# Where a block's results wait on their way out: staging them in the attention output's buffer

## The chip, the cores and the metric

The kernel runs on one core of a Trainium2 chip. The metric is device time in microseconds (us) of one execution. Engines go by the profile's names: PE is TensorE (PEld its weight loads), DVE is VectorE, ACT is ScalarE, POOL is GpSimd, SP is the engine that issues the DMAs.

## What is computed

Three stages follow one another. First an attention over 4 batches of 8 heads: 512 local tokens each attend to a window of 32 tokens to either side and to 32 global tokens, and the 32 global tokens attend to all 544. Its 2176 rows of 512 then go through two feed-forward networks.

```python
x = attn_out.transpose(0, 2, 1, 3).reshape(2176, 512)
h = x @ w_in                                   # 512 x 2048
x = where(h > 0, h, exp(min(h, 0)) - 1) @ w_out
xn = x / sqrt(mean(x * x, -1) + 1e-6) * rms_g
out = (silu(xn @ w_gate) * (xn @ w_val)) @ w_o2   # 512 x 1536, 1536 x 512
```

Products are made in three passes of a 32-bit format, a value being split into a high and a low part (ScalarE casts the high part, VectorE subtracts it to get the low one).

## The kernel before

**Blocks.** The local tokens are four blocks, one per batch, of 512 columns each. `moe_block(b, slot)` (L312) runs block b of the first network in 16 chunks j of 128 hidden units. In each chunk `mm1` (L126) makes h with 12 matmuls, the slot function calls `act1` (L136), which makes e and from it g, and `mm2` (L143) adds the previous chunk's g to four results y0 to y3 in PSUM (12 matmuls, two halves of 6). The last chunk's `mm2` and the store of the block's results are carried into the next block's chunk 0 (`finish_block`, L305; `store_y`, L152); for block 3 they follow its loop (L899).

**Attention beside it.** While block b runs, `att_slot` (L287) does the attention of block b + 1, one tile of 128 tokens per four chunks: scores and exponentials (`a_S`, `a_E`) in the first, transposes (`a_T`, ptp and ET) in the second, the product with V and its normalisation (`a_PV`, `a_N`) in the third. `a_N` writes the result x into a tile of tag x32 that is asked for at the block's first tile (L264); its writes are L272. In chunk 15 `a_X` (L274) transposes x into the next block's input xT. The slots also decode the second network's weights (L83, L90 to L93, L483 to L486), which go back to DRAM by small stores (L459). In block 3 the slot function `slot3` (L854) does the global tokens' attention instead; it collects its output in xg32, a tile of tag x32 (L779, written by `g_X`, L852), and from chunk 10 on runs the global tile through the first network, summing it in gg["y"], a PSUM tile.

**Result store.** Four evictions in turn, ScalarE for 0 and 2 into tag stg, VectorE for 1 and 3 into tag e, and a DMA after each:

```python
if dc % 2:
    t = moe.tile([P, 512], F32, tag="e", name="yev", bufs=2)
    nc.vector.tensor_copy(t[:, :n], ys[dc][:, :n])
else:
    t = stg.tile([P, 512], F32, tag="stg", name="yev")
    nc.scalar.copy(t[:, :n], ys[dc][:, :n])
nc.sync.dma_start(out=yT[:, dc, t0:t0 + n], in_=t[:, :n])
```

**Buffers.** Tiles of one pool and tag share its buffers and get them in the order in which the program asks; whoever writes a new tile waits until all readers of the buffer's last one are done, a DMA among them. Tag e has two buffers, which hold the e of `elu` and `elu_a` (L112, L120) as well; stg has two; x32 has one; xT3 has one and holds a quarter of xT in the blocks and sq2, the squares for the second network's norm (L611), behind them.

**After block 3.** The global tile's sum is copied to ysb (L901, tag stg), transposed (`g_finish`, L718, tile ygt), copied again (L723, tag stg) and stored. Then the second network runs in three chunks of columns: `product` (L726, tiles A and Q) makes the gate and value products from weights that `split` (L571) prepares, `o_mm` (L735) the last one. The norm's sums for the next chunk are acc (L609, tag stg) and sq (L614), and L625 sums them over partitions.

**Order.** TensorE's instructions run in the order of the program. Those of the other engines and of SP, which issues every DMA and waits in order for what each needs, are ordered when the kernel is built, by a planner that works with an estimated timeline and the program's order as priority. `e`, `yev`, `x` and the others in the profile are the tiles' names.

Of the kernel before, what the change touches and what calls it, by code (L numbers as in the profile page):

```python
# [7 lines left out]
F32 = mybir.dt.float32  # L8
# [13 lines left out]
P = 128  # L22
# [20 lines left out]
def fused_kernel(ctx: ExitStack, tc: tile.TileContext, kq, vl, gkq, gv, w_in, w_out, w_gate, w_val, w_o2, rms_g, consts, out):  # L43
    nc = tc.nc
# [5 lines left out]
    stg = ctx.enter_context(tc.tile_pool(name="stg", bufs=2))  # L50
    moe = ctx.enter_context(tc.tile_pool(name="moe", bufs=1))
# [6 lines left out]
    ident = cpool.tile([P, P], F32, name="ident")  # L58
# [3 lines left out]
    yT = dram.tile([P, 4, NT], F32, name="yT")  # L62
# [87 lines left out]
        return [yps.tile([P, 512], F32, tag=f"y{i}", name=f"y{i}") for i in range(4)]  # L150

    def store_y(ys, t0, n):  # L152
        for dc in range(4):
            if dc % 2:
                t = moe.tile([P, 512], F32, tag="e", name="yev", bufs=2)
                nc.vector.tensor_copy(t[:, :n], ys[dc][:, :n])
            else:
                t = stg.tile([P, 512], F32, tag="stg", name="yev")
                nc.scalar.copy(t[:, :n], ys[dc][:, :n])
            nc.sync.dma_start(out=yT[:, dc, t0:t0 + n], in_=t[:, :n])  # L160


    SETS = ("A11", "A12", "S2", "S1", "S3", "A22", "S4")
# [14 lines left out]
    with ExitStack() as ls:  # L178
# [126 lines left out]
        def finish_block(dcs=range(4)):  # L305
            ys, g, t0, n = carry[0]
            mm2(ys, g, 15, n, dcs)
            if dcs[-1] == 3:
                store_y(ys, t0, n)
                carry.clear()  # L310
# [379 lines left out]
    def second_mm2(i):  # L690
        if i == 0:
            gg["y"] = aps.tile([P, 512], F32, tag="att", name="yg")
        if 0 <= i < 4:
            g_mm2(gg["y"], gg.pop(i), i)
# [21 lines left out]
    gg = {}  # L716

    def g_finish(ysb):  # L718
        pt = aps.tile([P, 512], F32, tag="att", name="ygt")
        for i in range(4):  # L720
            nc.tensor.transpose(pt[:, i * P:(i + 1) * P], ysb[:, i * P:(i + 1) * P], ident)
        yt = stg.tile([P, 512], F32, tag="stg", name="yev")
        nc.scalar.copy(yt, pt)  # L723
        nc.sync.dma_start(out=yT[:, :, 16 * P:17 * P], in_=yt.rearrange("p (c t) -> p c t", c=4))

    def product(ps, k, i, pos, m, first=True):  # L726
        n, q = sizes[k], 14 * i + 2 * pos + m
# [48 lines left out]
    xg = xgp.tile([P, 4, 2, P], F32R, name="xg")  # L776
    with ExitStack() as gs:
        gp = gs.enter_context(tc.tile_pool(name="gp", bufs=1))
        xg32 = moe.tile([P, 4, 512], F32, tag="x32", name="xg32")  # L779
        zero = gp.tile([P, 64], F32, name="zero")[:, 0:1]  # L780
        nc.vector.memset(zero, 0.0)
        G = {}

        def g_load_k(b):
            if b < 4:
                r = gp.tile([P, 4 * S + 4 * SG], F32, tag="gkq", name="gkq")
                nc.sync.dma_start(out=r, in_=gkq[b])  # L790
                for par in range(2):
                    G[2 * b + par] = {"k": r[:, :4 * S].rearrange("p (a n) -> p a n", a=4), "q": r[:, 4 * S:].rearrange("p (a n) -> p a n", a=4)}

        def g_load_v(u):
            if u < 8:
                r = gp.tile([P, 5, 256], F32, tag="gvr", name="gvr", bufs=2)
                nc.sync.dma_start(out=r, in_=gv[u])
                G[u]["v"] = r

        def g_S(b, n):  # L800
            ds = [G[2 * b + par] for par in range(2)]
            if n == 0:
                for d in ds:
                    d["st"] = small.tile([P, 8], F32, tag="st", name="gst")
                    d["p"] = gp.tile([P, 576], F32, tag="gp", name="gpp", bufs=4)[:, :S]
            ss = [aps.tile([P, 272], F32, tag="att", name="gs") for par in range(2)]
            for a in range(4):
                for par in range(2):
                    r = slice(64 * par, 64 * par + 64)
                    nc.tensor.matmul(ss[par][32 * a:32 * a + 32, :], ds[par]["q"][r, a, :], ds[par]["k"][r, a, n * 272:(n + 1) * 272], start=True, stop=True)  # L810
            for par in range(2):
                nc.vector.tensor_tensor_reduce(out=ds[par]["p"][:, n * 272:(n + 1) * 272], in0=ss[par], in1=zero.to_broadcast([P, 272]), scale=-SCALE, scalar=3.0e38,
                                               op0=ALU.add, op1=ALU.min, accum_out=ds[par]["st"][:, n:n + 1])
            if n == 1:
                for d in ds:
                    st, p = d["st"], d["p"]
                    nc.vector.tensor_tensor(out=st[:, 3:4], in0=st[:, 0:1], in1=st[:, 1:2], op=ALU.min)
                    nc.scalar.activation(p, p, AF.Exp, bias=st[:, 3:4], scale=-1.0, accum_out=st[:, 4:5])
                    nc.vector.tensor_scalar(out=st[:, 6:7], in0=st[:, 4:5], scalar1=1e-9, scalar2=None, op0=ALU.add)
                    nc.vector.reciprocal(st[:, 7:8], st[:, 6:7])  # L820

        def g_T(u):
            d = G[u]
            p = d["p"]
            pa = aps.tile([P, 512], F32, tag="att", name="gpa")
            pb = aps.tile([P, P], F32, tag="att", name="gpb")
            for c in range(4):
                nc.tensor.transpose(pa[:, c * P:(c + 1) * P], p[:, c * P:(c + 1) * P], ident)
            nc.tensor.transpose(pb[:32, :], p[:, 512:544], ident)
            pt = gp.tile([P, 640], F32, tag="gpt", name="gpt", bufs=2)  # L830
            nc.scalar.copy(pt[:, :512], pa)
            nc.vector.tensor_copy(pt[:32, 512:640], pb[:32, :])
            d["pt"] = pt

        def g_PV(u):
            d = G[u]
            o = aps.tile([P, 64], F32, tag="att", name="go")
            for c in range(5):
                r = P if c < 4 else 32
                for a in range(4):  # L840
                    nc.tensor.matmul(o[32 * a:32 * a + 32, :], d["pt"][:r, c * P + 32 * a:c * P + 32 * a + 32], d["v"][:r, c, 64 * a:64 * a + 64],
                                     start=(c == 0), stop=(c == 4))
            e = gp.tile([P, 64], F32, tag="ge", name="ge", bufs=2)
            nc.vector.tensor_scalar(out=e, in0=o, scalar1=d["st"][:, 7:8], scalar2=None, op0=ALU.mult)
            d["e"] = e

        def g_X(u):
            d = G.pop(u)
            b, par = u // 2, u % 2
            x = aps.tile([P, P], F32, tag="att", name="gx")  # L850
            nc.tensor.transpose(x[:64, :], d["e"], ident)
            nc.scalar.copy(xg32[64 * par:64 * par + 64, :, b * 32:b * 32 + 32], x[:64, :].rearrange("d (a q) -> d a q", a=4))  # L852

        def slot3(j, part, h):  # L854
            g = act1(h, 512) if part == 0 else None
            b = j // 2
            if j < 8:
                if j % 2 == 0:
                    if part < 2:
                        g_S(b, part)  # L860
                    elif b:
                        g_PV(2 * b - 1)
                        g_load_v(2 * b + 1)
                        g_X(2 * b - 2)
                elif part < 2:
                    g_T(2 * b + part)
                else:
                    g_load_k(b + 1)
                    g_PV(2 * b)
                    g_load_v(2 * b + 2)  # L870
                    if b:
                        g_X(2 * b - 1)
            elif j == 8 and part == 2:
                g_PV(7)
                g_X(6)
            elif j == 9 and part == 0:
                g_X(7)
                nc.scalar.copy(xg[:, :, 0, :], xg32[:, :, :P])
                nc.vector.tensor_tensor(out=xg[:, :, 1, :], in0=xg32[:, :, :P], in1=f(xg[:, :, 0, :]), op=ALU.subtract)
            elif j == 9 and part == 2:  # L880
                gs.close()
                second_start()
            if j >= 10:
                if part == 0:
                    if 0 <= j - 11 < 4:
                        gg[j - 11] = g_act(gg.pop("e"))
                    if j - 12 < 3:
                        second_mm2(j - 12)
                    second_mm1(j - 10)
                if part == 2:  # L890
                    second_slot(j - 10)
            return g

        g_load_k(0)
        g_load_v(0)
        g_load_v(1)
        moe_block(3, slot3)
        second_mm2(3)
        finish_block()  # L899
    ysb = stg.tile([P, 512], F32, tag="stg", name="ysb")  # L900
    nc.vector.tensor_copy(ysb, gg["y"])  # L901
    split()
    g_finish(ysb)
    stage.close()
# [3 lines left out]
    for k in range(3):  # L908
        n = sizes[k]
# [163 lines left out]
```

## Time and profile before

| | |
|---|---|
| runs of the kernel | 912.31 us median of 3 (911.75 to 914.02) |
| profiled execution, device time | 914.21 us |
| its span, first to last instruction | 912.3 us |
| mean granted clock of TensorE | 0.983 |
| DVE busy, ACT busy | 587.0 us (64%), 476.0 us (52%) |
| moved by DMA | 139.27 MB |

A line of the timeline has the start, the duration, the engine, the line of the kernel, the operation and out<-in; in square brackets stands the idle time of the engine just before and what ended it. SPq is SP issuing a DMA, and the duration there is the issue, not the transfer. A line of a window has the stretch, its length and each engine's busy time in it. In the chain of what ended last each piece has its start, its length and its kind; a DMA there is the time from issue to landing.

### The profile page before, as it was taken

The numbers are of one execution on the slowest core, as the hardware profiler recorded it, in microseconds if no ns is written. First come the engines' busy times: TensorE is split into PE (matmuls) and PEld (weight loads), VectorE is DVE, ScalarE is ACT, GpSimd is POOL, SyncE is SP. The second block draws the span as 40 slices with busy tenths as digits, with TensorE's granted clock in tenths as the row PEclk, the third lists the DMA queues.
The fourth block names the chain that finished last, engine by engine and source line by source line (L and its number), as shares of the span: only waits on it lengthen the run. The fifth ranks groups of instructions, "written<-read, shape, count | busy, mean of one in ns | idle before, by whom it ended". The sixth has DMA issues, their size and how long they took to land.

```text
span 912.3 us, 16268 instructions
## 1 busy us (share of the span) xinstructions
PE 870.9 (95%) x6652; PEld 741.3 (81%) x6652; DVE 587.0 (64%) x983; ACT 476.0 (52%) x863; POOL 18.5 (2%) x22
## 2 busy tenths in 40 slices
PE   4789999899999999999999799999999999999996
PEld 3567877688887888777888699997999998899985
DVE  4899978667678763543489455886355786365642
ACT  4677664345454544333456456665445665355531
POOL 0000000000000000000110100000100100000000
PEclk8999999899999999999999899999999999999999
DMA  9785365766686862351405532243122333133200
GB/s 361 279 300 203 124 239 176 260 206 220 223 300 216 256 198 110 128 191 59 165 1 184 172 94 93 93 136 118 58 93 93 113 98 102 52 123 116 93 24 35
DMA packets 60370, 139.27 MB, mean 153 GB/s; under 512 B 5000, under 2 KB 30728, under 8 KB 57736
## 3 DMA queue, kind: packets, MB, share of 16 engines
q1 hardware_dynamic: 60296, 138.24, 44.0%
q8 instruction: 52, 0.85, 0.4%
q14 instruction: 22, 0.18, 0.1%
HBM read 115.15 MB, written 23.07 MB: 152 GB/s over the span
## 4 chain that ended last, share of the span: by engine, by line
PE 75%; DVE 10%; DMA 8%; ACT 3%; issue 2%; SPq 1%; ACTq 0%; DVEq 0%
PE A L732 16%; PE o L738 15%; PE y L146 13%; PE h L132 13%; PE Q L732 11%; DMA yT<-yev 2%; DMA kq<-in_kq 2%; DMA raw<-in_moe_w_in 2%; DVE dx L92 2%; DVE dx L93 1%; PE o L257 1%; PE ptp L244 1%; DVE dx L90 1%; PE s L226 1%; PE hg L667 1%
## 5 line engine op out<-in xcount | busy, mean ns | idle before, releaser
L146 PE MATMUL y<-g,wA 128*128 128x512 f32 x768 | 200.5, 404 | 7.0 <-DVE g L140 5.2
L132 PE MATMUL h<-xT,wA 128*128 128x512 f32 x768 | 186.9, 392 | 1.7 <-DVE xT L282 1.7
L146 PEld LDWEIGHTS y<-g,wA 128*128 128x128 f32 x768 | 141.6, 191 | 43.8 <-DVE g L140 8.2
L132 PEld LDWEIGHTS h<-xT,wA 128*128 128x128 f32 x768 | 143.9, 189 | 32.9 <-DVE xT L282 2.4
L732 PE MATMUL A<-xc,wS 128*128 128x384 f32 (+1 forms) x864 | 156.8, 330 | 0.0
L732 PEld LDWEIGHTS A<-xc,wS 128*128 128x128 f32 x864 | 146.5, 189 | 3.9
L738 PE MATMUL o<-wB,p 128*128 128x512 f32 x612 | 147.4, 392 | 0.8 <-ACT p L742 0.3
L738 PEld LDWEIGHTS o<-wB,p 128*128 128x128 f32 x612 | 113.6, 188 | 24.8 <-DVE p L743 2.4
L732 PE MATMUL Q<-xc,wS 128*128 128x384 f32 (+1 forms) x648 | 115.3, 326 | 0.0
L732 PEld LDWEIGHTS Q<-xc,wS 128*128 128x128 f32 x648 | 107.8, 188 | 0.0
L587 DVE TENSOR_TENSOR wS<-wraw,wS 128x1024 fp32r<-128x1024 f32 x63 | 77.7, 1233 | 36.6 <-ACT wS L586 36.5
L747 DVE TENSOR_TENSOR t<-t,Q 128x384 f32<-128x384 f32 (+1 forms) x108 | 55.8, 527 | 39.4 <-PE Q L732 28.9
L586 ACT CAST wS<-wraw 128x1024 fp32r<-128x1024 f32 x63 | 65.9, 1050 | 18.8 <-PE Q L732 11.9
L139 ACT CAST g<-e 128x512 fp32r<-128x512 f32 x64 | 39.8, 622 | 53.7 <-DVE e L123 37.2
L121 ACT ACTIVATE e<-h 128x512 f32<-128x512 f32 x48 | 29.0, 605 | 72.1 <-PE h L132 63.6
L123 DVE SCALAR_TENSOR_TENSOR e<-e,h 128x512 f32<-128x512 f32 x48 | 32.5, 678 | 40.7 <-ACT e L122 40.7
L140 DVE TENSOR_TENSOR g<-e,g 128x512 fp32r<-128x512 f32 x64 | 43.7, 683 | 9.1 <-ACT g L139 8.8
L743 DVE TENSOR_TENSOR p<-p,p 128x384 fp32r<-128x384 f32 x36 | 19.9, 556 | 43.3 <-ACT p L742 43.3
L83 ACT ACTIVATE dx<-raw 128x1024 f32<-128x1024 f32 x34 | 39.3, 1158 | 16.2 <-DMA raw<-in_moe_w_gate 5.5
L90 DVE TENSOR_SCALAR dx<-dx 128x1024 f32<-128x1024 f32 x34 | 23.3, 689 | 34.2 <-ACT dx L83 34.0
L238 ACT ACTIVATE E<-s,mx 128x128 f32<-128x128 f32 x128 | 34.8, 385 | 17.1 <-DVE mx L236 17.1
L92 DVE SCALAR_TENSOR_TENSOR dx<-raw,dx 128x1024 int32<-128x1024 int32 x34 | 41.9, 1238 | 0.6
(173 smaller groups left out, 869.5 us busy)
## 6 DMA issues: line engine op xcount, KB each, us to landing
wraw<-wS SPq DMA_DIRECT2D x63, 512.0 KB, 3.3
raw<-in_moe_w_out SPq DMA_DIRECT2D x14, 1024.0 KB, 8.7
raw<-in_moe_w_in SPq DMA_DIRECT2D x8, 1024.0 KB, 6.2
raw<-in_moe_w_gate SPq DMA_DIRECT2D x6, 1024.0 KB, 6.1
raw<-in_moe_w_val SPq DMA_DIRECT2D x6, 1024.0 KB, 6.8
wS<-raw SPq DMA_DIRECT2D x48, 128.0 KB, 2.6
gvr<-in_gv SPq DMA_DIRECT2D x8, 640.0 KB, 4.0
wS<-dx SPq DMA_DIRECT2D x36, 128.0 KB, 2.1
```

The source lines that it names most:

```text
L83: ins = nc.scalar.activation(x, f(words(raw)[:, :, 1]), AF.Abs)
L92: nc.vector.scalar_tensor_tensor(out=i32(x), in0=word[:, :, 1], scalar=-0x40000000, in1=i32(x), op0=ALU.bitwise_and, op1=ALU.bitwise_or)
L132: nc.tensor.matmul(h[:, :n], W1[c, G][:, ws, o:o + P], xT[c][:, xs, :n], start=(k == 0), stop=(k == 11))
L139: nc.scalar.copy(g[:, 0, :n], e[:, :n])
L140: nc.vector.tensor_tensor(out=g[:, 1, :n], in0=e[:, :n], in1=f(g[:, 0, :n]), op=ALU.subtract)
L146: nc.tensor.matmul(ys[dc][:, :n], W2[j][:, ws, dc * P:(dc + 1) * P], g[:, gs, :n], start=(j == 0 and k == 0), stop=(j == 15 and k == 2))
L238: nc.scalar.activation(e[par][:, pr, :], ss[par][:, pr, :], AF.Exp, bias=mx[:, par, pr:pr + 1], scale=SCALE)
L586: nc.scalar.copy(t[:, :, 0, :], raw)
L587: nc.vector.tensor_tensor(out=t[:, :, 1, :], in0=raw, in1=f(t[:, :, 0, :]), op=ALU.subtract)
L732: nc.tensor.matmul(ps[:, :n], w[:, 2 * (q % 4) + c, ws, :], x[:, c, xs, :n], start=(first and c == 0 and z == 0), stop=(c == 1 and z == 2) ...
L738: nc.tensor.matmul(o, p[:, pp, t * P:(t + 1) * P], Wo[j][:, ww, :], start=(first and z == 0), stop=(last and z == 2))
L747: nc.vector.tensor_tensor(out=t, in0=t, in1=ps, op=ALU.add)
```

## The change

The results of blocks 0 to 2 (t0 below 1536) are evicted into one tile of tag x32 and leave by one DMA of 1 MB; block 3's leave as before. xg32 is asked for at its first use in `g_X`, behind block 2's store, instead of ahead of block 3. The global tile's sum goes into a tile of tag xT3, its copy stands ahead of `finish_block` in the program, and the transposed copy goes into the second half of the same tile.

```diff
--- before.py
+++ after.py
@@ -150,14 +150,22 @@
         return [yps.tile([P, 512], F32, tag=f"y{i}", name=f"y{i}") for i in range(4)]
 
     def store_y(ys, t0, n):
+        t = moe.tile([P, 4, 512], F32, tag="x32", name="yev") if t0 < 1536 else None
         for dc in range(4):
+            if t is not None:
+                o = t[:, dc]
+            elif dc % 2:
+                o = moe.tile([P, 512], F32, tag="e", name="yev", bufs=2)
+            else:
+                o = stg.tile([P, 512], F32, tag="stg", name="yev")
             if dc % 2:
-                t = moe.tile([P, 512], F32, tag="e", name="yev", bufs=2)
-                nc.vector.tensor_copy(t[:, :n], ys[dc][:, :n])
+                nc.vector.tensor_copy(o, ys[dc])
             else:
-                t = stg.tile([P, 512], F32, tag="stg", name="yev")
-                nc.scalar.copy(t[:, :n], ys[dc][:, :n])
-            nc.sync.dma_start(out=yT[:, dc, t0:t0 + n], in_=t[:, :n])
+                nc.scalar.copy(o, ys[dc])
+            if t is None:
+                nc.sync.dma_start(out=yT[:, dc, t0:t0 + n], in_=o)
+        if t is not None:
+            nc.sync.dma_start(out=yT[:, :, t0:t0 + n], in_=t)
 
 
     SETS = ("A11", "A12", "S2", "S1", "S3", "A22", "S4")
@@ -718,10 +726,9 @@
     def g_finish(ysb):
         pt = aps.tile([P, 512], F32, tag="att", name="ygt")
         for i in range(4):
-            nc.tensor.transpose(pt[:, i * P:(i + 1) * P], ysb[:, i * P:(i + 1) * P], ident)
-        yt = stg.tile([P, 512], F32, tag="stg", name="yev")
-        nc.scalar.copy(yt, pt)
-        nc.sync.dma_start(out=yT[:, :, 16 * P:17 * P], in_=yt.rearrange("p (c t) -> p c t", c=4))
+            nc.tensor.transpose(pt[:, i * P:(i + 1) * P], ysb[:, 0, i * P:(i + 1) * P], ident)
+        nc.scalar.copy(ysb[:, 1], pt)
+        nc.sync.dma_start(out=yT[:, :, 16 * P:17 * P], in_=ysb[:, 1].rearrange("p (c t) -> p c t", c=4))
 
     def product(ps, k, i, pos, m, first=True):
         n, q = sizes[k], 14 * i + 2 * pos + m
@@ -776,7 +783,6 @@
     xg = xgp.tile([P, 4, 2, P], F32R, name="xg")
     with ExitStack() as gs:
         gp = gs.enter_context(tc.tile_pool(name="gp", bufs=1))
-        xg32 = moe.tile([P, 4, 512], F32, tag="x32", name="xg32")
         zero = gp.tile([P, 64], F32, name="zero")[:, 0:1]
         nc.vector.memset(zero, 0.0)
         G = {}
@@ -847,6 +853,9 @@
         def g_X(u):
             d = G.pop(u)
             b, par = u // 2, u % 2
+            if u == 0:
+                G["x"] = moe.tile([P, 4, 512], F32, tag="x32", name="xg32")
+            xg32 = G["x"]
             x = aps.tile([P, P], F32, tag="att", name="gx")
             nc.tensor.transpose(x[:64, :], d["e"], ident)
             nc.scalar.copy(xg32[64 * par:64 * par + 64, :, b * 32:b * 32 + 32], x[:64, :].rearrange("d (a q) -> d a q", a=4))
@@ -875,6 +884,7 @@
                 g_X(6)
             elif j == 9 and part == 0:
                 g_X(7)
+                xg32 = G["x"]
                 nc.scalar.copy(xg[:, :, 0, :], xg32[:, :, :P])
                 nc.vector.tensor_tensor(out=xg[:, :, 1, :], in0=xg32[:, :, :P], in1=f(xg[:, :, 0, :]), op=ALU.subtract)
             elif j == 9 and part == 2:
@@ -896,9 +906,9 @@
         g_load_v(1)
         moe_block(3, slot3)
         second_mm2(3)
+        ysb = moe.tile([P, 2, 512], F32, tag="xT3", name="ysb")
+        nc.vector.tensor_copy(ysb[:, 0], gg["y"])
         finish_block()
-    ysb = stg.tile([P, 512], F32, tag="stg", name="ysb")
-    nc.vector.tensor_copy(ysb, gg["y"])
     split()
     g_finish(ysb)
     stage.close()
```

## Rows read from the trace of the kernel before

**Rows 1.** The page, its first and fourth part: busy time, and the chain that ended last

```profile
PE 870.9 (95%) x6652; PEld 741.3 (81%) x6652; DVE 587.0 (64%) x983; ACT 476.0 (52%) x863; POOL 18.5 (2%) x22
...
PE 75%; DVE 10%; DMA 8%; ACT 3%; issue 2%; SPq 1%; ACTq 0%; DVEq 0%
```

**Rows 2.** Windows: stretch, then length and busy (x instructions) by engine, clock, DMA share, GB/s

```profile
154.17:186.09 31.92, 29.08 (x242) 22.75 (x242) 18.49 (x32) 13.36 (x26) 0.00 (x0) 0.89 0.69 224
264.50:291.25 26.75, 25.81 (x242) 20.66 (x242) 18.89 (x31) 14.41 (x27) 0.00 (x0) 1.00 0.74 283
186.09:211.63 25.54, 25.54 (x242) 20.66 (x242) 18.30 (x30) 13.56 (x25) 0.00 (x0) 1.00 0.68 234
366.80:389.70 22.90, 22.90 (x228) 15.95 (x228) 11.72 (x40) 7.87 (x15) 0.00 (x0) 1.00 0.45 141
502.65:515.42 12.77, 6.52 (x29) 6.55 (x30) 3.16 (x4) 4.56 (x7) 3.00 (x3) 0.73 0.64 218
```

**Rows 3.** Timeline of ScalarE, first chunks of block 1

```profile
160.18 0.64 ACT L159 COPY yev<-y 128x512 f32<-128x512 f32 x1
160.65 1.19 ACT L83 ACTIVATE dx<-raw 128x1024 f32<-128x1024 f32 x1
167.84 0.60 ACT L121 ACTIVATE e<-h 128x512 f32<-128x512 f32 x1 [6.00 <-DMA yT<-yev]
```

**Rows 4.** Timeline of SP, first chunks of block 1

```profile
158.57 0.37 SPq L75 DMA_DIRECT2D raw<-in_moe_w_val  x1
159.50 2.25 SPq L160 DMA_DIRECT2D yT<-yev  x4
178.47 5.45 SPq L459 DMA_DIRECT2D wS<-raw  x8
```

**Rows 5.** The chain in order of time, first chunks of block 1

```profile
161.28 7.49 DMA yT<-yev
```

**Rows 6.** Timeline of ScalarE and VectorE, block 2, and ScalarE, block 3

```profile
274.62 0.60 ACT L121 ACTIVATE e<-h 128x512 f32<-128x512 f32 x1 [2.45 <-DMA yT<-yev]
...
284.72 0.75 DVE L272 TENSOR_TENSOR x<-o,st 128x256 f32<-128x256 f32 x2
...
390.67 0.24 ACT L852 COPY xg<-gx 64x128 f32<-64x128 f32 x1
```

**Rows 7.** Timeline of four engines, end of block 3

```profile
494.50 0.93 ACT L614 ACTIVATE sq<-ya 128x384 f32<-128x384 f32 x2
...
499.77 2.88 PE L146 MATMUL y<-g,wA 128*128 128x512 f32 x12
...
508.06 0.69 DVE L901 COPY ysb<-yg 128x512 f32<-128x512 f32 x1 [3.07 <-DMA yT<-yev]
...
508.89 1.09 PE L721 MATMUL ygt<-ident,ysb 128*128 128x128 f32 x4 [6.25 <-DVE ysb L901]
...
510.55 0.53 ACT L609 ACTIVATE acc<-ya 128x384 f32<-128x384 f32 x1
```

**Rows 8.** The chain in order of time, end of block 3

```profile
502.17 5.79 DMA yT<-yev
...
515.42 2.08 PE A L732 x12
```

**Rows 9.** Timeline of TensorE, first chunks of block 1

```profile
164.77 2.88 PE L132 MATMUL h<-xT,wA 128*128 128x512 f32 x12
```

**Rows 10.** Timeline of VectorE, first chunks of block 1

```profile
169.48 0.69 DVE L123 SCALAR_TENSOR_TENSOR e<-e,h 128x512 f32<-128x512 f32 x1 [4.93 <-ACT e L122]
...
171.88 0.69 DVE L140 TENSOR_TENSOR g<-e,g 128x512 fp32r<-128x512 f32 x1
...
178.15 0.75 DVE L272 TENSOR_TENSOR x<-o,st 128x256 f32<-128x256 f32 x2
```

**Rows 11.** DMA issues, 156 to 176: count, KB each, median us to landing

```profile
raw<-in_moe_w_val SPq DMA_DIRECT2D x1, 1024.0 KB, 5.3
```

**Rows 12.** The line L625 from 505 to 620: duration ns, first and last start

```profile
L625 PE MATMUL ms<-acc,ones x4: 485/486/486, 565.3 to 585.1; 128*128 128x384 f32 x4
```

## The prediction

> **What bounds the kernel now.** I read the page first. TensorE is busy 95% of the span, and the chain that ended last is 75% TensorE, 10% VectorE, 8% DMA [rows 1]. So a change that computes nothing less can only win where TensorE stands still or runs at its lower clock, and the question is where that is and whether a result store stands behind it. The windows answer it [rows 2]. In the middle of a block four chunks take 25.54 us with TensorE busy throughout at a granted clock of 1.00. The same four chunks, when they are the first of block 1, take 31.92 us, and as the first of block 2 they take 26.75 us. They hold the same work, as the matmul counts 242, 242 and 242 show. The excess is 6.38 us and 1.21 us. At block 1 TensorE's busy time is 29.08 us, so 2.84 us of the excess is idle and 3.54 us is the lower level of the clock (a mean of 0.89). At block 3 the matching stretch is wholly busy, 22.90 of 22.90 us at clock 1.00, so there is nothing to win.
>
> The timeline of ScalarE says what is late. At block 1 it ends a weight decode at 160.65 + 1.19 = 161.84 and then stands 6.00 us until a store of yev lands; only then does the next e (L121) start [rows 3]. The reason is in the code: two of the four staging tiles of store_y are taken from tag e, which has two buffers, so the next e needs the buffer of a store that is still under way. The stores are issued from 159.50 on, behind a weight load at 158.57 [rows 4], and the last is on the chain for 7.49 us, until 168.77 [rows 5]. At block 2 the same wait is 2.45 us [rows 6]; there TensorE has enough queued to hide most of it.
>
> The fourth place is the end of block 3. The last y matmuls end at 499.77 + 2.88 = 502.65, and the transposes of ygt start at 508.89 after 6.25 us of idle time [rows 7]. They wait for ysb, which VectorE copies at 508.06 after 3.07 us of waiting for a store [rows 7]; that store is on the chain from 502.17 for 5.79 us [rows 8]. Here ysb wants a buffer of tag stg, whose two buffers hold results on their way out. The window 502.65 to 515.42 holds four transposes and two groups of 12 products [rows 2]. One such group takes 2.08 us at clock 1.00 [rows 8], and four transposes about half of their 1.09 us, which ran at the lower clock; so the work is 0.55 + 2 x 2.08 = 4.71 us, and 12.77 - 4.71 = 8.06 us are lost, of which 6.2 us idle and the rest clock.
>
> **The change, part by part.** *Results of blocks 0 to 2 in x32.* The four evictions stay, on the same engines and with the same shapes (0.64 us for ScalarE's second at 160.18 [rows 3]); only their target moves. No new e waits for a store. At block 1 the e could start at 161.84, 6.00 us sooner, its h being done by then, since TensorE was well before the next one at 164.77 [rows 9]. Then VectorE's e (L123), 169.48 before, and the g that the next y needs (L140, 171.88 before) come 6 us sooner, at about 163.5 and 165.9 [rows 10]. TensorE ends its h at 164.77 + 2.88 = 167.65 [rows 9], so g is there in time, with some 1 us to spare after its 0.69 us. ScalarE's second decode lies between e and g; its weights were asked for at 158.57 [rows 4] and land 5.3 us later [rows 11], at 163.9, and the decode needs 1.2 us, so it too ends in time, but without much room. I therefore take back 5.4 of the 6.38 us at block 1 and 0.9 of the 1.21 us at block 2, and keep the whole and nothing as bounds.
>
> *One store for four.* Four issues cost SP 2.25 us in all [rows 4]; one is bounded by a single 256 KB issue (0.56 us) and by those 2.25 us. SP is on no critical path there, so I count nothing. But the one store cannot leave before the fourth eviction is done, 160.18 + 0.64 = 160.82, while the first of the four left at 159.50. What stands behind it on SP in this stretch is only later loads. The bytes are the same and the queue is full, so I take its landing to be where the last of the four landed, 168.77 [rows 5]; bounds are 0.5 us sooner and 2 us later.
>
> *The new wait that this brings.* x32 has one buffer. The attention's result for the next block but one (x, L272) goes into it, so L272 now waits for the 1 MB store, and VectorE's whole queue waits behind it: g, e and the decode. Before, L272 ran at 178.15 [rows 10]; with the 6.00 us gone it is due at about 172.2. The landing at 168.77 leaves 3.4 us. At block 2 it ran at 284.72, 10 us after the e at 274.62, whose start shows the store of its buffer landed [rows 6]. In block 3 the first write to xg32, which is now allocated after the store, is ScalarE's at 390.67 [rows 6], 24 us after the block's first chunk began at 366.8 [rows 2]. So the cost is nothing, hidden by the decode that stands before L272 on VectorE; where that cover fails it is the third rival.
> The Trainium skill (DMA: Bandwidth & Descriptors, section Anatomy of one DMA) fits a transfer by about 2.0 us plus its bytes at 436 GB/s. By that page 1 MB would be out 4.4 us after 160.82, at 165.2, and the margin would be 7 us; the rows do not agree, since a quarter of the bytes took 7.49 us in a loaded queue, and the measured landing stands in the sum. The third rival would be less likely by the page.
>
> *ysb in tag xT3, its copy written ahead of finish_block.* yg is complete when the y matmuls start at 499.77. VectorE can copy it between its weight splits, in 0.69 us [rows 7], before 502.65 in most orders; it may push an eviction back by 0.69 us, which nobody waits for. The transposes then follow the y matmuls directly and the products follow them, without the idle time behind which the clock was at its lower level. That is worth the 8.06 us as an upper bound.
> Two buffers pass to other waits, though. With ysb and the last yev gone from stg, acc of the next chunk (L609, 510.55 before [rows 7]) is the next in that tag, after the yev store that lands at 507.96 [rows 8]. And the squares sq2, of which ScalarE wrote two at 494.50 [rows 7], now come after ysb in tag xT3, so they wait for the store of ysb's second half. Their results are only needed by TensorE's L625 at 565.3 [rows 12], so they are not urgent themselves. The queue behind them is: if ScalarE stands at acc until 508.0, the copies of the first products (L921) stand behind. The products start at about 503.2, and after four groups of half-sets, 4.16 us, TensorE needs those copies, at 507.4; the two copies (0.5 us each) would end at 509. That would cost 1.6 us, and standing at sq2 up to 3.5 us. I take 1.0 us and expect 7.0 of the 8.06 us.
>
> **Sum.** 5.4 + 0.9 + 7.0 = 13.3 us. The profiled execution took 914.21 us (span 912.3), so it would become 900.9; it lies 1.9 us above the median of the runs shown, 912.31. Against that median I predict 899.0 us. With everything taken back (15.65 us) it is 896.7. Behind each of the four places TensorE is the bound, wholly busy in the windows of a block's middle and at block 3 [rows 2] and back to back in the products [rows 8], so what is won early stays won.
>
> **Rivals.** *First: block 1 gives nothing back.* ScalarE's next decode or VectorE's backlog takes the place of the store. For it: the decode has 1 us of room, and VectorE is 10% of the chain [rows 1]. Against it: VectorE itself stood idle before L123 at 169.48 for 4.93 us [rows 10]. Time: 899.0 + 5.4 = 904.4.
> *Second: the end wait changes its owner.* ScalarE stands at acc or sq2 with the copies behind it, 3.5 us rather than 1.0: 901.5, and at most 4.5 us back, so 903.
> *Third, slower.* The order of SP, ScalarE and VectorE is planned at build from an estimated timeline, so the 1 MB store may be put behind work that is blocked, such as the put group that SP issues from 178.47 to 183.92 [rows 4]. It would then leave at 184 and land some 6 us later (between 5.79 and 7.49 [rows 5, 8]), at 190. L272 would hold VectorE from 172 to 190, and TensorE, which the g already made feeds for three groups of 2.7 us, would stand from about 181 to 190.5. That is 9.5 us at each of blocks 1 and 2, with 3.5 us of clock behind each (as block 1 lost now), in place of the 6.38 and 1.21 us of now [rows 2]: 912.3 - 7.0 + 2 x 13.0 - 7.6 = 923.7. It turns the sum against the change when each of the two stands costs 8.7 us with its clock, which is a landing at about 186. Against it: before, the stores leave within 2 us of the evictions at all three boundaries.
> *Fourth: nothing happens,* since the planner's new order gives elsewhere what is won here: 912.
>
> **How the numbers follow.** The forecast has 0.64, the first rival 0.10, the second 0.12, the third 0.07, the fourth 0.07. The range reaches from everything taken back, less the 1 us by which the runs shown spread downward (895.5), to the first rival and a little of it together with the second (906.5); that leaves out the third and the fourth and a part of what may come from a new order. A measurement of this kernel can tell 0.3% (2.7 us) from no change. Faster by more than that takes the forecast, the first and second rivals and a part of the fourth: 0.88; same 0.05; slower 0.07.
>
> **What would show it.** Right: no wait of e (L121) for yT at 161.84, the first four chunks of block 1 in about 26.5 us at clock 1.00, ygt directly behind the last y, L272 without a DMA wait. Wrong: a DMA wait before L272 or acc with TensorE idle behind it; a first stretch of block 1 still near 32 us, then with a weight load or the decode as what ends the wait; the 1 MB store late on SP.

## The result, and the profile after

The changed kernel takes 898.9 us (median of 5 runs, 897.99 to 901.6) against 912.31 us for the kernel before (5 runs, 911.6 to 914.16). The ratio is 0.9853, with a 95% interval of 0.9834 to 0.9872. The forecast was 899.0 us.

The profiled execution took 899.1 us with a span of 897.3 us, 15.0 us under that of before. Its page answers to [rows 1]; TensorE's share rises, and the DMA part of the chain is halved:

```profile
PE 864.9 (96%) x6652; PEld 736.4 (82%) x6652; DVE 588.0 (66%) x983; ACT 475.8 (53%) x863; POOL 19.4 (2%) x22
...
PE 79%; DVE 11%; DMA 4%; ACT 3%; issue 1%; SPq 0%; POOL 0%; ACTq 0%
```

The windows answer to [rows 2], cut at the same instructions (first scores to the scores four chunks on for blocks 1 and 2; the whole stretch of block 3). Columns are as there.

```profile
153.19:178.75 25.56, 25.56 (x242) 20.66 (x242) 18.37 (x32) 13.48 (x26) 0.00 (x0) 1.00 0.83 271
257.16:282.70 25.54, 25.54 (x242) 20.66 (x241) 19.50 (x33) 14.48 (x27) 0.00 (x0) 1.00 0.78 292
...
358.30:381.20 22.90, 22.90 (x228) 15.97 (x227) 11.68 (x40) 7.92 (x15) 0.00 (x0) 1.00 0.42 143
```

Block 1's first four chunks take 25.56 us in place of 31.92, block 2's 25.54 in place of 26.75, both with TensorE busy throughout at clock 1.00. Block 3's stretch is what it was, 22.90 us. The timeline of block 1, all engines, shows the wait gone:

```profile
159.21 0.64 ACT L164 COPY yev<-y 128x512 f32<-128x512 f32 x1
159.68 1.20 ACT L83 ACTIVATE dx<-raw 128x1024 f32<-128x1024 f32 x1
159.87 0.65 SPq L168 DMA_DIRECT2D yT<-yev  x1
...
160.69 0.68 ACT L121 ACTIVATE e<-h 128x512 f32<-128x512 f32 x1
...
165.84 0.69 DVE L140 TENSOR_TENSOR g<-e,g 128x512 fp32r<-128x512 f32 x1
...
172.13 0.75 DVE L280 TENSOR_TENSOR x<-o,st 128x256 f32<-128x256 f32 x2
```

ScalarE starts e (L121) at 160.69, as the decode before it is ending, with no wait for yT; before it stood there 6.00 us [rows 3]. The 1 MB store leaves at 159.87, 0.02 us after the last eviction (159.21 + 0.64). Its landing is not in the profile's lists (the page's 5.5 us for such stores is the one issued at 366.57, in block 3); the last of its 16 completion events in the trace is at 167.34, 7.47 us after the issue. The attention's result x (now L280) is written at 172.13, 4.8 us later, and VectorE waits for no store there. The end of block 3 answers to [rows 7]:

```profile
491.25 2.88 PE L146 MATMUL y<-g,wA 128*128 128x512 f32 x12
...
493.27 0.68 DVE L910 COPY ysb<-yg 128x512 f32<-128x512 f32 x1
...
494.01 0.66 PE L729 MATMUL ygt<-ident,ysb 128*128 128x128 f32 x4
...
495.76 0.48 ACT L931 COPY t<-A 128x384 f32<-128x384 f32 x1
...
499.90 0.52 ACT L617 ACTIVATE acc<-ya 128x384 f32<-128x384 f32 x1 [3.65 <-DMA yT<-yev]
500.33 0.46 ACT L931 COPY t<-A 128x384 f32<-128x384 f32 x1
500.81 1.28 ACT L937 ACT_TABLE_LOAD   x1
...
500.84 1.32 PE L739 MATMUL A<-xc,wS 128*128 128x384 f32 x6 [0.94 <-ACT t L931]
...
502.10 0.53 ACT L937 ACTIVATE t<-t 128x384 f32<-128x384 f32 x1
502.53 1.04 ACT L594 CAST wS<-wraw 128x1024 fp32r<-128x1024 f32 x1
...
503.47 0.93 ACT L622 ACTIVATE sq<-ya 128x384 f32<-128x384 f32 x2
...
504.31 0.46 ACT L946 COPY t<-A 128x384 f32<-128x384 f32 x1
...
504.82 2.36 PE L739 MATMUL A<-xc,wS 128*128 128x384 f32 x12 [0.56 <-ACT t L946]
...
509.47 2.35 PE L739 MATMUL A<-xc,wS 128*128 128x384 f32 x12 [0.20 <-ACT t L952]
```

VectorE copies ysb at 493.27 without a wait, and the transposes of ygt start at 494.01, 0.04 us after the y matmuls' issue slots end (12 x 0.227 us behind 491.25); 6.25 us stood there before. Then comes what was won less: acc (now L617) waits 3.65 us for a yev store, and the copy of the second product tile (L931 at 500.33) stands behind it on ScalarE. TensorE meets gaps of 0.94, 0.56 and 0.20 us at its next product groups.

Where the time went, from the two profiles. The last length runs from block 3's last y matmuls to the product group behind the first `o_mm`:

| stretch | before | after | difference |
|---|---|---|---|
| start to block 1's first scores | 154.17 | 153.19 | -0.98 |
| block 1, first four chunks | 31.92 | 25.56 | -6.36 |
| block 2, first four chunks | 26.75 | 25.54 | -1.21 |
| end of block 3, 499.77 to 523.58 and 491.25 to 509.47 | 23.81 | 18.22 | -5.59 |
| start of the span to the last eviction | 905.58 | 891.42 | -14.16 |

The first line is not the change's: nothing in block 0 differs (each engine's instructions stand in the same order up to block 1's first stores), and the twelve profiles of this study have block 1's first scores anywhere from 152.60 to 155.00 (154.85 in late_copy, whose program is the changed kernel's). The other 0.84 us of the span lie behind the last eviction, in the last stores' way out.

### The profile page after: what moved, and what is told of

The parts are those of the page before. It is cut to its first block, busy times and chain, and to the rows that moved or that the text cites. A ratio compares the mean times of both kernels' runs of the same rounds, so it can differ in the third digit from the quotient of the medians.

```text
span 897.3 us, 16243 instructions
## 1 busy us (share of the span) xinstructions
PE 864.9 (96%) x6652; PEld 736.4 (82%) x6652; DVE 588.0 (66%) x983; ACT 475.8 (53%) x863; POOL 19.4 (2%) x22
## 4 chain that ended last, share of the span: by engine, by line
PE 79%; DVE 11%; DMA 4%; ACT 3%; issue 1%; SPq 0%; POOL 0%; ACTq 0%
PE y L146 16%; PE A L739 15%; PE h L132 15%; PE o L745 15%; PE Q L739 11%; DMA kq<-in_kq 2%; DVE dx L93 2%; DVE dx L92 1%; PE s L234 1%; PE ptp L252 1%; DVE wA L99 1%; PE o L265 1%; PE hg L675 1%; DMA raw<-in_moe_w_out 1%; DVE dx L90 1%
## 5 line engine op out<-in xcount | busy, mean ns | idle before, releaser
L146 PE MATMUL y<-g,wA 128*128 128x512 f32 x768 | 197.3, 400 | 4.7 <-DVE g L140 4.1
L121 ACT ACTIVATE e<-h 128x512 f32<-128x512 f32 x48 | 29.0, 605 | 69.8 <-PE h L132 69.7
```

The source lines that it names most:

```text
L146: nc.tensor.matmul(ys[dc][:, :n], W2[j][:, ws, dc * P:(dc + 1) * P], g[:, gs, :n], start=(j == 0 and k == 0), stop=(j == 15 and k == 2))
```

## The experiments

All times are medians; the ratio is to the kernel before on the same chip. The two kernels of the last two lines have one run each.

| kernel | us | before | ratio (95%) |
|---|---|---|---|
| x32_only | 905.95 | 911.63 | 0.9940 (0.9926 to 0.9954) |
| sum_only | 906.32 | 911.63 | 0.9946 (0.9926 to 0.9967) |
| three_e | 906.81 | 911.63 | 0.9950 (0.9935 to 0.9965) |
| four_stores | 899.68 | 911.63 | 0.9870 (0.9855 to 0.9885) |
| acc_free | 898.84 | 912.83 | 0.9848 (0.9829 to 0.9866) |
| acc_free2 | 897.79 | 912.83 | 0.9840 (0.9822 to 0.9858) |
| late_copy | 900.38 | 912.83 | 0.9870 (0.9851 to 0.9888) |
| early_stg | 901.91 | 912.83 | 0.9885 (0.9866 to 0.9904) |
| store_x3 | 902.58 | 914.62 | one run |
| store_x5 | 940.24 | 914.62 | one run |

**x32_only: the first part alone.** From the changed kernel, the second part undone:

```diff
-        ysb = moe.tile([P, 2, 512], F32, tag="xT3", name="ysb")
-        nc.vector.tensor_copy(ysb[:, 0], gg["y"])
         finish_block()
+    ysb = stg.tile([P, 512], F32, tag="stg", name="ysb")
+    nc.vector.tensor_copy(ysb, gg["y"])
     split()
...
+        yt = stg.tile([P, 512], F32, tag="stg", name="yev")
+        nc.scalar.copy(yt, pt)
+        nc.sync.dma_start(out=yT[:, :, 16 * P:17 * P], in_=yt.rearrange("p (c t) -> p c t", c=4))
```

> The first part alone: results of blocks 0 to 2 in x32 with one store, xg32 asked for late; ysb and its copy as in the kernel before. Theory (the next e was held up by a yev store that still read its buffer): both block stretches return to 25.5 us, so 7.6 us less than before, about 904.7 us, and the 6.2 us of idle TensorE ahead of ygt stay. Rival (the two parts lean on each other, for instance through the planner's order): clearly less than 7.6 us, or a wait for yT at another place.

Its windows for blocks 1 and 2:

```profile
153.12:178.73 25.61, 25.61 (x243) 20.67 (x242) 18.38 (x32) 13.47 (x26) 0.00 (x0) 1.00 0.84 268
257.14:282.68 25.54, 25.54 (x242) 20.66 (x241) 19.60 (x33) 14.48 (x27) 0.00 (x0) 1.00 0.78 293
```

Both stretches are free of waits, as expected. The kernel is 5.7 us faster, not 7.6. In its profile the end of block 3 costs 1.0 us more than before: from the last y to the product group behind the first `o_mm` it is 24.80 us in place of 23.81. Of that, 0.4 us is ysb, which waits 3.45 us for its store in place of 3.07; the rest is the clock behind the stop (the transposes and the first two product groups take 6.97 us at a mean clock of 0.64, before 6.37 us at 0.70). With 6.31 and 1.21 us won that leaves 6.5 us in the profiles; the runs spread over 2.8 us, those of the kernel before over 3.8 us.

**sum_only: the second part alone.** From the kernel before:

```diff
+        ysb = moe.tile([P, 2, 512], F32, tag="xT3", name="ysb")
+        nc.vector.tensor_copy(ysb[:, 0], gg["y"])
         finish_block()
-    ysb = stg.tile([P, 512], F32, tag="stg", name="ysb")
-    nc.vector.tensor_copy(ysb, gg["y"])
     split()
...
-        yt = stg.tile([P, 512], F32, tag="stg", name="yev")
-        nc.scalar.copy(yt, pt)
+        nc.scalar.copy(ysb[:, 1], pt)
```

> The second part alone: the global tile's sum in xT3 and its copy ahead of the last stores; blocks 0 to 2 store as in the kernel before. Theory (ysb waited for a stg buffer): the idle time ahead of ygt goes from 6.2 us to under 0.5 us, some 1.7 us come back as a wait of the product groups behind acc, net 5.5 us less than before, about 906.8 us; block 1's first four chunks stay at 32 us. Rival (what is won there comes from the earlier part): 911 to 912 us.

It is 5.3 us faster. The end takes 18.14 us, as in the changed kernel, and ygt follows the last y without idle time. Block 1 keeps most of its loss (30.62 us, where 32 were expected; the clock is 0.94 there and was 0.89 before), as its windows for blocks 1 and 2 show:

```profile
155.00:185.62 30.62, 27.61 (x242) 21.63 (x242) 18.50 (x32) 13.39 (x26) 0.00 (x0) 0.94 0.73 232
264.03:290.09 26.06, 25.83 (x241) 20.66 (x241) 18.18 (x31) 14.20 (x27) 0.00 (x0) 1.00 0.75 287
```

Its list of waits (in total, times, longest) has the e that stood there:

```profile
ACT e L121 <- DMA yT<-yev: 7.8, 2, 6.0
```

So the two parts add up within the noise: 5.7 and 5.3 us alone, 12.0 us together on the same chip (four_stores, below). The 1.0 us between is less than the intervals can tell, so it is not shown that the parts lean on each other, and a small dependence is not excluded.

**three_e: a third e buffer and nothing else.** From the kernel before, all six tiles of the tag:

```diff
-                t = moe.tile([P, 512], F32, tag="e", name="yev", bufs=2)
+                t = moe.tile([P, 512], F32, tag="e", name="yev", bufs=3)
```

> The kernel before with a third buffer for tag e and nothing else: four stores per block, the same staging tiles. Theory (it was the held e buffer): the e of block 1's chunk 1 finds a free buffer, its first four chunks take 25.5 to 26.5 us, block 2's 25.5; 905 us, close to the first part alone. Rival (the gain is that of one large store in place of four, fewer issues and fuller transfers): the four stores are unchanged here, so 912 us.

Its windows for blocks 1 and 2:

```profile
152.79:178.35 25.56, 25.56 (x242) 20.66 (x242) 18.38 (x32) 13.47 (x26) 0.00 (x0) 1.00 0.84 264
256.76:282.30 25.54, 25.54 (x241) 20.66 (x241) 20.19 (x34) 14.59 (x27) 0.00 (x0) 1.00 0.79 297
```

ScalarE's timeline of the same kernel, at the e of chunk 1:

```profile
159.27 1.19 ACT L83 ACTIVATE dx<-raw 128x1024 f32<-128x1024 f32 x1
160.29 0.67 ACT L121 ACTIVATE e<-h 128x512 f32<-128x512 f32 x1
```

Four small stores, e's own buffers, no large store, and the loss is gone all the same: 25.56 and 25.54 us. The e starts as the decode at 159.27 is ending. This shows the cause: it was the buffer that a store still read. It is 4.8 us faster in the runs, at 906.81 us where 905 was expected; its end takes 25.25 us, 1.4 us more than before, with ysb waiting 3.46 us and the clock at a mean of 0.60 behind.

**four_stores: x32, but a store per quarter.** From the changed kernel:

```diff
-            if t is None:
-                nc.sync.dma_start(out=yT[:, dc, t0:t0 + n], in_=o)
-        if t is not None:
-            nc.sync.dma_start(out=yT[:, :, t0:t0 + n], in_=t)
+            nc.sync.dma_start(out=yT[:, dc, t0:t0 + n], in_=o)
```

> The changed kernel, but each quarter of the x32 tile leaves by its own 256 KB store behind its eviction, as before the change. Theory (the buffer, not the number of stores): 899 us, the same as the changed kernel within 0.3%, since SP has time for four issues. Rival (one store is worth something by itself): up to 906 us, with the block stretches longer than 25.5 us.

```profile
153.43:178.99 25.56, 25.56 (x242) 20.66 (x242) 18.35 (x32) 13.49 (x26) 0.00 (x0) 1.00 0.85 266
257.40:282.94 25.54, 25.54 (x241) 20.66 (x241) 19.94 (x33) 14.59 (x27) 0.00 (x0) 1.00 0.79 296
```

Both stretches and the time are those of the changed kernel (0.9870 and 0.9853, intervals overlapping). One store in place of four is worth nothing that these runs can tell.

**acc_free and acc_free2: what is left at the end.** From the changed kernel; the second line of the second part is acc_free2's alone:

```diff
         t = moe.tile([P, 4, 512], F32, tag="x32", name="yev") if t0 < 1536 else None
+        u = moe.tile([P, 2, 512], F32, tag="xT2", name="yev") if t is None else None
...
-                o = stg.tile([P, 512], F32, tag="stg", name="yev")
+                o = u[:, dc // 2]
...
-        ysb = moe.tile([P, 2, 512], F32, tag="xT3", name="ysb")
+        ysb = moe.tile([P, 2, 512], F32, tag="g", name="ysb", bufs=2)
```

> The changed kernel, with block 3's first and third result staged in a tile of tag xT2 (free until the product stage's t3) in place of stg, so that acc finds a free stg buffer. Theory (the 3.65 us that ScalarE stands at acc, with a product copy behind it, cost TensorE the 1.7 us of gaps at its next product groups): those gaps go, 1.5 to 1.7 us less than the changed kernel, about 897.3 us. Rival (the wait only moves on, to the squares behind ysb's store in tag xT3): the gaps come back some 3 us later, 898.5 to 900 us.

> As acc_free, and ysb in tag g in place of xT3, so that the squares of the next chunk can run early, as in the kernel before. Theory: the same 897.3 us, or 0.3 us less than acc_free if the squares stood in the way there. Rival (the squares' early run or the g buffer takes ScalarE or VectorE time that the products need): 898 us or more.

The timeline of acc_free around the squares:

```profile
503.54 0.94 ACT L623 ACTIVATE sq<-ya 128x384 f32<-128x384 f32 x2 [1.84 <-DMA yT<-ysb]
...
504.90 2.37 PE L740 MATMUL A<-xc,wS 128*128 128x384 f32 x12 [0.24 <-ACT t L947]
```

The window of acc_free2 from ygt to the product group behind the first `o_mm` (15.46 us with 1.71 us idle in the changed kernel, 494.01 to 509.47):

```profile
495.64:508.58 12.94, 12.94 (x74) 12.55 (x73) 8.48 (x13) 9.12 (x15) 0.00 (x0) 1.00 0.84 266
```

In acc_free acc no longer waits, and the rival is right about where the wait goes: ScalarE stands 1.84 us at the squares until ysb's store lands. TensorE loses 0.24 us by it. From the last y on, this end takes 16.21 us (492.98 to 509.19), 2.0 us less than the changed kernel. In acc_free2 that is gone too: 12.94 us, wholly busy at clock 1.00, and 16.03 us from the last y (492.55 to 508.58). The 18.22 us of the changed kernel thus hold 2.2 us of waits behind acc; against late_copy, which is the same program (next) and whose profile has 17.57 us there with acc waiting 3.09 us, it is 1.5 us. acc_free's median of 898.84 us lies in the rival's range as it was written, but on its own chip it is 1.5 us below late_copy, as the theory said, and the runs don't overlap. On the one chip acc_free2 ran at 897.02 to 898.24 us and late_copy at 899.43 to 902.38: the medians are 2.6 us apart and the runs don't overlap. It has the lowest median of the study.

**late_copy: the copy written behind the stores.** From the changed kernel:

```diff
-        ysb = moe.tile([P, 2, 512], F32, tag="xT3", name="ysb")
-        nc.vector.tensor_copy(ysb[:, 0], gg["y"])
         finish_block()
+    ysb = moe.tile([P, 2, 512], F32, tag="xT3", name="ysb")
+    nc.vector.tensor_copy(ysb[:, 0], gg["y"])
     split()
```

> The changed kernel, with ysb in xT3 but its copy written behind the last stores, as before the change. Theory (the buffer is what counts; the copy then runs behind both evictions, TensorE stands some 1.5 to 2 us at ygt, but acc is held until the same store lands, so the later gaps shrink by as much): 899 to 900 us, within 0.3% of the changed kernel at its lower end. Rival (the order counts by itself): 1.5 to 2 us more than the changed kernel, 900.5 us or more.

VectorE's timeline at the end of block 3:

```profile
494.47 0.68 DVE L911 COPY ysb<-yg 128x512 f32<-128x512 f32 x1
495.07 0.68 DVE L162 COPY yev<-y 128x512 f32<-128x512 f32 x1
```

The copy of ysb still runs ahead of both evictions. Each engine's instructions stand in the same order as in the changed kernel, one by one; the planner places the copy by when it is ready, and the place in the text changed nothing. So neither expectation could be tested, and the run is a second timing of the changed kernel: 0.9870 (0.9851 to 0.9888) beside 0.9853.

**early_stg: the copy written sooner, but in stg.** From the changed kernel:

```diff
-        ysb = moe.tile([P, 2, 512], F32, tag="xT3", name="ysb")
-        nc.vector.tensor_copy(ysb[:, 0], gg["y"])
+        ysb = stg.tile([P, 512], F32, tag="stg", name="ysb")
+        nc.vector.tensor_copy(ysb, gg["y"])
         finish_block()
...
+        yt = stg.tile([P, 512], F32, tag="stg", name="yev")
+        nc.scalar.copy(yt, pt)
```

> The changed kernel, with the copy of ysb ahead of the last stores but in tag stg, and the transposed copy in stg too, as before the change. Theory (the buffer is what counts): ygt follows the last y with under 1 us of idle time, but its copy waits for the first result's store, which holds both ScalarE and the buffer that the second Q tile needs; TensorE stands about 3 us there, 900 to 902 us. Rival (writing the copy sooner is enough): 899 us, like the changed kernel.

```profile
501.78 0.58 ACT L731 COPY yev<-ygt 128x512 f32<-128x512 f32 x1 [4.09 <-DMA yT<-yev]
...
502.42 1.74 PE L740 MATMUL Q<-xc,wS 128*128 128x384 f32 x6 [3.16 <-ACT yev L731]
```

The copy of ygt waits 4.09 us for a yev store on ScalarE, and the second Q tile waits 3.16 us for its buffer. From the last y on the end takes 20.66 us (492.79 to 513.45) against 18.22, and 17.57 in late_copy. The time, 901.91 us, is what the theory gave, but its runs overlap those of late_copy on the same chip (899.43 to 902.38), so it is the profile that speaks against the rival. With ysb in stg the place of the copy does count: it takes its buffer ahead of the two evictions and waits for nothing, and the end costs 4.1 us less than in x32_only (24.80 us), but the copy of ygt waits in its stead. With a chunk's tile for both the place counts for nothing (late_copy).

**store_x3 and store_x5: how far off the new wait is.** From the changed kernel, three or five stores of the same 1 MB:

```diff
-            nc.sync.dma_start(out=yT[:, :, t0:t0 + n], in_=t)
+            for _ in range(3):
+                nc.sync.dma_start(out=yT[:, :, t0:t0 + n], in_=t)
```

> The changed kernel, with each block's 1 MB store issued three times, so that x32 is held longer. In the changed kernel the store lands near 165.4 and x (L280) is written at 172.1, a margin of 6.7 us. Theory: two more stores at about 2.6 us each bring the last landing to about 171, still ahead of x; block 1's and block 2's first four chunks stay at 25.5 to 26 us. Rival (the new wait is near): L280 waits for a store, and a stretch grows by more than 1 us.

> The same with five stores, 4 MB more per block, landing near 176. Theory: x (L280) then waits for a store for about 4 us, on VectorE, with the next g behind it; TensorE has work in hand for about 8 us, so the two stretches grow by less than 2 us each. Rival (no cover): each stretch grows by the whole wait, 4 us or more. Loads asked for behind the stores land later too, which can add to either.

The chain of store_x3 in block 1 (start, us, what):

```profile
159.28 7.61 DMA yT<-yev
...
166.91 5.89 DMA yT<-yev
...
172.82 6.02 DMA yT<-yev
```

The timeline of store_x3 behind it:

```profile
178.96 0.76 DVE L281 TENSOR_TENSOR x<-o,st 128x256 f32<-128x256 f32 x2 [6.02 <-DMA yT<-yev]
...
179.44 0.62 PE L229 MATMUL s<-masks,identr 128*32 128x256 bf16 x8 [1.16 <-DVE x L281]
```

The timeline of store_x5 at the same place:

```profile
175.95 2.88 PE L132 MATMUL h<-xT,wA 128*128 128x512 f32 x12
...
193.61 0.76 DVE L281 TENSOR_TENSOR x<-o,st 128x256 f32<-128x256 f32 x2 [11.40 <-DMA yT<-yev]
...
194.09 0.73 PE L229 MATMUL s<-masks,identr 128*32 128x256 bf16 x8 [15.27 <-DVE x L281]
```

The windows of store_x5, the first four chunks of block 1 and the next four:

```profile
153.21:194.09 40.88, 25.62 (x241) 20.64 (x240) 19.57 (x34) 15.32 (x29) 0.00 (x0) 0.87 0.84 289
194.09:222.56 28.47, 28.47 (x241) 22.68 (x242) 18.10 (x29) 11.79 (x22) 0.00 (x0) 0.89 0.62 214
```

The chain of store_x5 has the last of its five stores, and SP's timeline what stands ahead of the fourth:

```profile
188.61 4.81 DMA yT<-yev
```

```profile
174.65 3.72 SPq L468 DMA_DIRECT2D wS<-dx  x4
178.47 4.93 SPq L468 DMA_DIRECT2D wS<-raw  x5
183.44 0.53 SPq L169 DMA_DIRECT2D yT<-yev  x1
```

The expectation was wrong about the landing, in two ways. It set out from a landing near 165.4 in the changed kernel, which was block 3's 5.5 us; the one at block 1 is at 167.34, and here too the first store takes 7.61 us. And the stores write the same rows of yT, and none goes out before the one ahead has landed; in store_x5 the fourth stands behind nine small weight stores on SP besides. So the last of three lands at 178.84 and the last of five at 188.61 + 4.81 = 193.42, not at 171 and 176. In store_x3 x waits 6.02 us, and TensorE stands 1.16 us at the next scores, which wait for x. The stretch grows to 26.84 us and the next to 26.23, 2.0 us in all. (Block 2 says the same: its first four chunks take 27.39 us in store_x3 and 41.63 us in store_x5.) In store_x5 TensorE stands 15.27 us at the scores and finds the clock lower behind it: 40.88 us at block 1 and 28.47 us for the next four chunks (28.47 of 28.47 busy, clock 0.89), 18.3 us in all. So the mechanism of the third rival is real, and its price grows about 1 for 1: from a landing of 178.84 to one of 193.42, 14.6 us later, the cost rises by 16.3 us, of which 2.9 are the clock. The changed kernel lands at 167.34, by this price an estimated 10 us short of where the loss begins (both counted from block 1's first scores).

## Why the prediction was right, point by point

**What bounds, and where.** TensorE is still the bound, and the places were the right ones: blocks 1 and 2 and the end of block 3 gave time back, block 3's start gave none.

**The held e buffer** was the cause at blocks 1 and 2, as three_e shows with one more buffer and x32_only with x32. The term was sized at 5.4 of 6.38 us and 0.9 of 1.21 us; it is 6.36 and 1.21. The reserve for the decode between e and g was not needed, though the decode did cost something: g came at 165.84, where 165.9 was worked out, but the whole block began 0.98 us sooner, so counted from its first scores g is 0.9 us later than that. TensorE took the first y with it at 167.66, 1.1 us after g's end.

**One store for four** was counted at nothing, and four_stores shows that. Its landing was taken as 168.77, as the last of four had landed; it is 167.34, which from the block's first scores is 14.15 us in place of 14.60, inside the bounds that were given. The Trainium skill (DMA: Bandwidth & Descriptors, section Anatomy of one DMA) has a fit, made for transfers that GpSimd issues, and the estimate by it was 4.4 us for 1 MB. The three stores here leave from SP and took 7.47, 4.27 and 5.47 us by their completion events (issued at 159.87, 263.84 and 366.57), so the trace agrees at block 2 alone; the measured values stand.

**The new wait at x** cost nothing, as said: x was due at 172.2 and ran at 172.13, 4.8 us after the landing, where 3.4 were expected. The agreement of the two times is luck in part: from the block's first scores x ran 0.9 us later than worked out.

**ysb.** The buffer was the cause at the end: with the copy written where it stood before, ysb waits 3.45 us in tag stg (x32_only) and not at all in xT3 (late_copy). Here is the term that was mis-sized: of 8.06 us the prediction expected 7.0 and 5.59 came. The wait at acc was named with its place, its landing store and the copies behind it, but 1.0 us was taken where the text itself had 1.6 as the price of that case. It cost 2.2 us (1.5 by late_copy's profile), as acc_free2 shows by taking it away: one product copy was already through when ScalarE stopped, but the gaps went on for three groups (0.94, 0.56, 0.20 us), and in that time ScalarE did the table load, the silu (L937), a weight split and two squares ahead of the next product copy (L946 at 504.31). What each of these added is not shown. The other wait that was feared, of the squares behind ysb's store, did not come: sq (L622) starts at 503.47 without one.

**The sum.** 5.4 + 0.9 + 7.0 = 13.3 us was expected, and 6.36 + 1.21 + 5.59 = 13.16 us is what the same stretches gave. The medians differ by 13.4 us. So the closeness to 899.0 owes something to two errors of opposite sign, 1.3 us too little at the blocks and 1.4 us too much at the end.

**The rivals.** The first (the decode takes the place of the store) did not occur. The second (the end wait changes its owner) occurred in part, at 2.2 us in place of the forecast's 1.0 and the rival's 3.5. The third did not occur, since the store leaves SP at once. Its sum breaks even at 7.3 us for each stand, (7.0 + 7.6) / 2; 8.7 us is where the kernel would be 2.7 us slower. Its price was wrong, too: TensorE was given 8 us of work in hand, up to 181, with g as what runs out first. In store_x3 and store_x5 it stood from 178.3 and 178.8 on, and what ran out was the scores, which wait for x to be written out of its source. And one part of the change does nothing beside the other tile: that the copy is written sooner, as late_copy shows.

## What to carry to other kernels

When an engine that feeds the bound one waits for a store, ask which buffer the store still reads and who is next in that tag: a larger tag, or a tile that is idle at that time, takes the wait away; the number of stores did not matter here (four_stores). Then follow the buffers that were freed and taken to their next users, since the wait goes to whoever is next in the tag with a transfer in front (acc here, then the squares), and price each by what stands behind it on its engine. Where a planner orders the engines, moving a line in the text may change nothing; look at the order before crediting it.

## What the runs showed that was not expected

A store that writes rows that an earlier store wrote waits in this program for the earlier one to land, 5.9 to 7.6 us each at block 1 of store_x3, so repeating a store there is a serial delay and not only a load on the queue. The landing of a 1 MB store depends on where it stands: 7.47, 4.27 and 5.47 us at the three blocks of the changed kernel.

TensorE's clock fell behind a stop of 15.27 us in store_x5 to a mean of 0.89 over the next 28.47 us, at a cost of 2.9 us, and behind the stop of 6.25 us in the kernel before. It fell behind short stops too: in block 1 of the kernel before they are 1.31, 0.34, 1.00 and 0.18 us within 4 us.

```profile
168.96 0.67 PE L257 MATMUL o<-v__1726,ET 128*32 128x65 f32 x32 [1.31 <-ACT ET L246]
...
171.64 0.80 PE L146 MATMUL y<-g,wA 128*128 128x512 f32 x1 [1.00 <-ACT g L139]
```

Behind them, from 172.62 to 178.00, TensorE was busy throughout at a granted clock of 0.50, the lower of its two levels (1.2 GHz). After the gaps of 0.94, 0.56 and 0.20 us of the changed kernel it stayed at 1.00 in the window from 494.01 to 509.47, and so it did around the stops of 1.16 and 1.78 us at the scores in store_x3. So the length of the longest stop alone does not tell whether the clock falls; what decides is not shown.
